# Moving one weight combination to another byte offset, and a smaller planner cost for a group of six products

## The chip, the cores and the metric

The kernel runs on one core of one Trainium2 chip, as one program. The metric is device time in microseconds (us) of one execution. Engines are named as in the profile: PE is TensorE's matmul, PEld its weight load, DVE is VectorE, ACT is ScalarE, POOL is GpSimd, SP is SyncE, which issues most DMAs.

## The reference

Retention attention, a one-expert-per-token feed-forward layer, and a dense feed-forward layer, in float32. The change is in the last, `_moe2_ref`, on 4608 tokens with a model width of 512 and 2048 hidden units:

```python
h = np.maximum(x @ w_in, 0.0)
return (h * h @ w_out).astype(np.float32)
```

## The kernel before

`phase0` does the attention, `phase12` the expert layer and, beside it, the preparation of the dense layer's weights (into `wc` in device memory); `phase3` does the dense layer.

**The dense layer.** Each 2x2 block product is done with seven products instead of eight (a Strassen-Winograd form), on seven combinations of the activations (`XT[0..6]`), of the first weights (`w`, `MW` says which) and of the second weights. Every operand is split into a high and a low part (`hilo`, `split`), and a product is taken as high x high, high x low, low x high. `six` issues such a group: two triples of matmuls, each with 128 rows, a 128x128 weight and 256 columns. Its three matmuls stand in lines 1210, 1211 and 1212: the first two use the same high weight, the third the low weight. The expert layer's counterpart is `three` (lines 839 to 841), with up to 512 columns and 256 in its last, narrowest tile.

**Order of the work.** `PASSES` cuts the 2048 hidden units into eight slices of 256, taken as three passes of 3, 2 and 3 slices. In each pass all nine tiles of 512 tokens are done (in alternating direction). For a tile and a slice q of the pass, `one` gives seven groups (x = 1, 2, 6, 5, 7, 4, 3 in that order for a slice; the slices overlap by the numbers in `AT1`), then come the squares on ACT and DVE and the splitting into `h`; `two` gives seven groups for each slice with `h` as the weight. That is 9 x (3 + 2 + 3) x 7 x 2 = 1008 groups, 6048 matmuls.

**The planner.** `Plan.add` records every operation with its engine, an assumed duration and the keys that it reads and writes; `Plan.emit` is a list scheduler. It puts a due time on each operation from the sum of the assumed PE durations, walks an assumed clock forward, and so fixes the order in which each engine's queue receives its work (and for the squares which of DVE and ACT does them). Nothing of the assumed times remains at run time: the engines run their queues in that order and wait on semaphores. The assumed duration of a group is `MMS`, 0.72 us; a DMA's is its size over 320 plus 2.0 us.

**Layout.** For the first weights one tile per slice and half (x = 0 high, x = 1 low) holds seven combinations of 256 columns (1024 bytes) in a row. The view starts 16 floats, 64 bytes, after the tile's start. The activations `XT`, which are the moving operand beside them, start at the tile's start. All these tiles start a whole number of 256 bytes apart. So within every 128 bytes the weights of `one` start 64 bytes off the moving operand. In `two` the weights are `h`, whose view starts 56 floats in so as to be 64 bytes off likewise, and the moving operand is the second weight at a tile's start. In the expert layer (`wx`, `wy` against `xh`, `hh`) weights and moving operand both start at byte 0 in this sense. Below, "byte 64" and "byte 0" name these two cases.

**Weights' transfers.** `wload2` loads the first pass's early slices at the end of `phase12`, `loadw` the rest. Each load of a first-weight tile is one DMA of 896 KB under one key, `("w", 0, q, x)`; a group of `one` waits for the keys of both halves.

Of the kernel before, what the change touches and what calls it, by code (L numbers as in the profile page):

```python
# [9 lines left out]
F32 = mybir.dt.float32  # L10
F32R = mybir.dt.float32r
# [14 lines left out]
P = 128  # L26
# [15 lines left out]
PASSES = ((0, 1, 2), (3, 4), (5, 6, 7))  # L42
# [50 lines left out]
def kernel(ctx, tc, qT, kT, kN, vN, modT, w_gate, mbias, w1, w2, w_in, w_out,  # L93
                              vdec_d, odec_d, mats_d, rows_d, out):
    nc = tc.nc
    pe, act, dve, pool, sp = nc.tensor, nc.scalar, nc.vector, nc.gpsimd, nc.sync
# [35 lines left out]
    wc = dram.tile([2, NFP, 2, P, 7 * 256], F32, name="wc")  # L132
# [933 lines left out]
    held = {}  # L1066

    def wload2(m, j, pool_, load=True):
        for x in range(2):
            if m:  # L1070
                held["w", m, j, x] = pool_.tile([P, 4, 2, 256], F32R, tag="w", name=f"w{m}{j}{x}")
                if load:
                    for a in range(2):
                        n = 4 - x
                        sp.dma_start(held["w", m, j, x][:, 0:n, a, :].bitcast(F32),
                                     wc[m, PASSES[0][j], a][:, x * 1024:x * 1024 + 256 * n]
                                     .rearrange("p (m c) -> p m c", c=256))
                continue
            wt = pool_.tile([P, 7 * 256 + 32], F32R, tag="w", name=f"w{m}{j}{x}")
            held["w", m, j, x] = wt[:, 16:16 + 7 * 256].rearrange("p (m c) -> p m c", m=7)  # L1080
            if load:
                sp.dma_start(held["w", m, j, x].bitcast(F32).rearrange("p m c -> p (m c)"), wc[m, PASSES[0][j], x])

    MX = {1: 0, 2: 1, 3: 2, 5: 3, 6: 4, 7: 5, 4: 6}
    MW = {1: 0, 4: 1, 2: 2, 5: 3, 6: 4, 7: 5, 3: 6}
# [71 lines left out]
    def phase3():  # L1157
        with ExitStack() as c2:
            ff = c2.enter_context(tc.tile_pool(name="ff", bufs=1))
            sb = lambda name, shape, dt=F32R: ff.tile(shape, dt, tag=name, name=name)  # L1160
            plan = Plan()
            for j in (1, 2):
                wload2(1, j, wp, False)
            WT = [[[held["w", m, j, x] for x in range(2)] for j in range(3)] for m in range(2)]
# [12 lines left out]
            PE_, ACT_, DVE_, POOL_, DMA_ = (Eng(n_, h_) for n_, h_ in  # L1177
                                            (("PE", pe), ("ACT", act), ("DVE", dve), ("POOL", pool), ("DMA", sp)))
# [5 lines left out]
            def copy(o, i, c, r, w, f=AF.Copy):  # L1184
                plan.add(a_(c), lambda e: e.activation(o, i, f), r, w)  # L1185

            def tt(o, a, b, op, c, r, w, engs=None):
                plan.add(engs or d_(c), lambda e: e.tensor_tensor(out=o, in0=a, in1=b, op=op), r, w)  # L1188

            def sq(z, c, k):  # L1190
                def go(e):
                    if e is act:
                        e.activation(z, z, AF.Relu)
                        e.activation(z, z, AF.Square)
                    else:
                        e.scalar_tensor_tensor(out=z, in0=z, scalar=0.0, in1=z, op0=ALU.max, op1=ALU.mult)  # L1196

                plan.add(d_(c) + [(ACT_, 2 * a_(c)[0][1])], go, k, k)

            def dma(o, i, kb, r, w, early=False):  # L1200
                plan.add(m_(kb), lambda e: (pool if early else e).dma_start(o, i), r, w, 2.0)
# [5 lines left out]
            def six(ps, pairs, first):  # L1207
                def go(e):
                    for n, ((lh, ll), (rh, rl)) in enumerate(pairs):
                        e.matmul(ps[n], lh, rh, start=first and n == 0, stop=False, skip_group_check=True)  # L1210
                        e.matmul(ps[n], lh, rl, start=False, stop=False, skip_group_check=True)  # L1211
                        e.matmul(ps[n], ll, rh, start=False, stop=True, skip_group_check=True)  # L1212
                return go

            MMS = [(PE_, 0.72)]

            def loadw(p, m, j0=0):
                for j, fp in list(enumerate(PASSES[p]))[j0:]:
                    for x in range(2):
                        if m:  # L1220
                            n = 4 - x
                            for a in range(2):
                                dma(WT[m][j][x][:, 0:n, a, :].bitcast(F32),
                                    wc[m, fp, a][:, x * 1024:x * 1024 + 256 * n].rearrange("p (m c) -> p m c", c=256),
                                    131 * n, [], [("w", m, j, x, a)])
                            continue
                        dma(WT[m][j][x].bitcast(F32).rearrange("p m c -> p (m c)"), wc[m, fp, x], 917,
                            [], [("w", m, j, x)])

            def xprep(n):  # L1230
                p, t = T3[n]
# [37 lines left out]
            def one(n, q, x):  # L1269
                p, t = T3[n]  # L1270
                if x == 1:
                    HS_[n, q] = cnt[0]
                    cnt[0] += 1
                u = HS_[n, q]
                X_, Y_, Z_ = (b_[:, 0:256] for b_ in (BX[u % 2], BY[u % 2], BZ))
                kx, ky, kz = ("X", u % 2), ("Y", u % 2), ("Z",)
                z, h = ZT[u % 3], HT[u % 3]
                kz_ = lambda *i: [("z", u % 3, j) for j in i]
                ps, kp = (X_, kx) if x in (1, 6, 7, 4) else ((Z_, kz) if x == 2 else (Y_, ky))
                w, m, mx = WT[0][q], MW[x], MX[x]  # L1280
                plan.add(MMS, six([ps, ps], [((w[0][:, m, P * k:P * k + P], w[1][:, m, P * k:P * k + P]),
                                              (XT[mx][:, 0, k, :], XT[mx][:, 1, k, :])) for k in range(2)],
                                  x in (1, 2, 5)),
                         [("w", 0, q, 0), ("w", 0, q, 1), ("x", mx, 0), ("x", mx, 1)], [kp])
                last = q == len(PASSES[p]) - 1
                if x == 1:
                    copy(z[:, 1, :], X_, 256, [kx], kz_(1))
                elif x == 2:
                    tt(z[:, 1, :], z[:, 1, :], Z_, ALU.add, 256, [kz] + kz_(1), kz_(1))
                    sq(z[:, 1, :], 256, kz_(1))  # L1290
                elif x == 6:
                    copy(z[:, 0, :], X_, 256, [kx], kz_(0))
                elif x == 7:
                    copy(z[:, 2, :], X_, 256, [kx], kz_(2))
                    tt(z[:, 2, :], z[:, 2, :], Y_, ALU.add, 256, [ky] + kz_(2), kz_(2))
                    sq(z[:, 2, :], 256, kz_(2))
                    if last:
                        hsplit(u, z, h, 0, 2, kz_)
                elif x == 4:
                    copy(z[:, 3, :], X_, 256, [kx], kz_(3), AF.Relu)  # L1300
                    copy(z[:, 3, :], z[:, 3, :], 256, kz_(3), kz_(3), AF.Square)
                    hsplit(u, z, h, 2 if last else 0, 3, kz_)
                elif x == 3:
                    tt(z[:, 0, :], z[:, 0, :], Y_, ALU.add, 256, [ky] + kz_(0), kz_(0))
                    sq(z[:, 0, :], 256, kz_(0))
                    tt(z[:, 4, :], z[:, 0, :], z[:, 2, :], ALU.add, 256, kz_(0, 2), kz_(4))
                    if last:
                        hsplit(u, z, h, 3, 4, kz_)
                    tt(z[:, 5, :], z[:, 4, :], z[:, 1, :], ALU.subtract, 256, kz_(4, 1), kz_(5))
                    hsplit(u, z, h, 4 if last else 3, 5, kz_)  # L1310
                    tt(z[:, 6, :], z[:, 1, :], z[:, 0, :], ALU.subtract, 256, kz_(1, 0), kz_(6))
                    tt(z[:, 7, :], z[:, 3, :], z[:, 5, :], ALU.subtract, 256, kz_(3, 5), kz_(7))
                    hsplit(u, z, h, 5, 7, kz_)

            def hsplit(u, z, h, a, b, kz_):
                rs = kz_(*range(a + 1, b + 1))
                ks = [[("h", u % 3, m, x) for m in range(a, b)] for x in range(2)]
                c = 256 * (b - a)
                plan.add(a_(c), lambda e: e.activation(h[:, 0, a:b], z[:, a + 1:b + 1], AF.Copy), rs, ks[0])  # L1319
                plan.add(d_(c), lambda e: e.tensor_tensor(out=h[:, 1, a:b], in0=z[:, a + 1:b + 1],  # L1320
                                                          in1=h[:, 0, a:b].bitcast(F32), op=ALU.subtract),
                         rs + ks[0], ks[1])
# [8 lines left out]
            def two(n, x):  # L1331
# [4 lines left out]
                for q in range(len(PASSES[p])):  # L1336
                    u = HS_[n, q]
                    h, m, w, mo = HT[u % 3], MH[x], WT[1][q], MO[x]
                    plan.add(MMS, six([ps[:, 0, :], ps[:, 1, :]],
                                      [((h[:, 0, m, P * b:P * b + P], h[:, 1, m, P * b:P * b + P]),  # L1340
# [108 lines left out]
```

## Time and profile before

| | |
|---|---|
| three runs | 1328.75, 1331.18, 1335.86 us (median 1331.18) |
| the profiled execution, its own time | 1336.03 us |
| its span, first to last instruction | 1334.2 us |
| mean granted TensorE clock | 0.995 |
| PE busy, PEld busy | 97%, 91% of the span |
| DVE, ACT, POOL busy | 77%, 47%, 9% |

The own time is the whole execution; the span is what the trace covers, 1.8 us less. Matmuls overlap each other in the pipeline, so a matmul's duration (280 ns) is longer than the distance from one start to the next, and a busy PE says nothing of its pace. The pace is read from starts.

### The profile page before, as it was taken

Reading aid. Unit: us, or ns where it says so; the run is one execution under the profiler, and the core shown is the slowest. Engines: PE = TensorE matmul, PEld = TensorE weight load, DVE = VectorE, ACT = ScalarE, POOL = GpSimd, SP = SyncE. Lnnn points to the kernel's source line nnn. Section 1 sums busy time; section 2 is a strip of 40 time slices with the busy share of each in tenths; the row PEclk is TensorE's granted clock in tenths of the full one; section 3 lists DMA queues with packets and bytes.
Section 4 is the critical chain, followed back from the end, with each engine's and each line's share of the span. In section 5 each row is a group of like instructions: output and inputs, shape, how many; then the busy total and the mean of one; then the engine's idle time right before and its main releaser. Section 6 shows DMA issues by size and latency. Waiting matters only on the chain.

```text
span 1334.2 us, 26978 instructions
## 1 busy us (share of the span) xinstructions
PE 1294.7 (97%) x10639; PEld 1209.6 (91%) x10639; DVE 1021.8 (77%) x2095; ACT 624.4 (47%) x1283; POOL 125.3 (9%) x170
## 2 busy tenths in 40 slices
PE   7999989999999999899999999999999999999997
PEld 6888877888888888899999999999999999999997
DVE  3877858878887887666888888858788777776765
ACT  2344444545445445455656566534334344443333
POOL 3222112101110110000000000000000011111121
PEclk9999999999999999899999999999999999999999
DMA  9998257787787877789555544778799766655551
GB/s 330 391 347 304 77 197 240 265 299 275 259 297 246 304 266 250 265 289 319 228 225 217 201 174 176 283 257 308 273 344 346 270 217 216 214 193 174 174 187 51
DMA packets 152499, 331.89 MB, mean 249 GB/s; under 512 B 15440, under 2 KB 67440, under 8 KB 152368
## 3 DMA queue, kind: packets, MB, share of 16 engines
q1 hardware_dynamic: 144752, 309.82, 65.5%
q0 software_dynamic: 5840, 19.14, 4.0%
q8 instruction: 85, 1.39, 0.4%
q10 hardware_dynamic: 1776, 1.17, 0.3%
q14 instruction: 46, 0.38, 0.1%
HBM read 222.33 MB, written 107.78 MB: 247 GB/s over the span
## 4 chain that ended last, share of the span: by engine, by line
PE 43%; DVE 10%; DMA 1%; issue 1%; POOL 0%; POOLq 0%; DVEq 0%
PE bank L1211 14%; PE bank L1210 14%; PE bank L1212 14%; DVE z L1188 4%; DVE h L1320 3%; DVE z L1196 1%; DVE x L1188 1%; DVE yr L1188 1%; DMA w<-wc 1%; DMA x<-xc 1%; PE bank L839 0%; PE bank L840 0%; PE bank L841 0%; POOL out L1327 0%; DVE oe L1188 0%
## 5 line engine op out<-in xcount | busy, mean ns | idle before, releaser
L1211 PE MATMUL bank<-x,w 128*128 128x256 f32 x1008 | 282.5, 280 | 4.2 <-DVE x L1188 4.2
L1210 PE MATMUL bank<-w,h 128*128 128x256 f32 x1008 | 282.1, 280 | 2.2 <-DVE oe L1188 1.6
L1210 PE MATMUL bank<-x,w 128*128 128x256 f32 x1008 | 281.9, 280 | 2.3 <-DMA x<-xc 2.3
L1212 PE MATMUL bank<-w,h 128*128 128x256 f32 x1008 | 282.1, 280 | 0.7 <-DVE h L1320 0.7
L1212 PE MATMUL bank<-x,w 128*128 128x256 f32 x1008 | 281.8, 280 | 0.9 <-DMA w<-wc 0.9
L1211 PE MATMUL bank<-w,h 128*128 128x256 f32 x1008 | 281.6, 279 | 0.0
L1185 ACT ACTIVATE z<-bank 128x256 f32<-128x256 f32 x288 | 108.6, 379 | 255.1 <-PE bank L1212 254.3
L1211 PEld LDWEIGHTS bank<-x,w 128*128 128x128 f32 x1008 | 189.3, 188 | 5.8 <-DVE x L1188 5.8
L1212 PEld LDWEIGHTS bank<-w,h 128*128 128x128 f32 x1008 | 191.9, 190 | 1.2 <-DVE h L1320 1.1
L1212 PEld LDWEIGHTS bank<-x,w 128*128 128x128 f32 x1008 | 191.9, 190 | 1.1 <-DMA w<-wc 1.1
L1210 PEld LDWEIGHTS bank<-w,h 128*128 128x128 f32 x1008 | 189.4, 188 | 2.9 <-DVE oe L1188 2.0
L1210 PEld LDWEIGHTS bank<-x,w 128*128 128x128 f32 x1008 | 189.4, 188 | 2.6 <-DMA x<-xc 2.5
L1319 ACT ACTIVATE h<-z 128x512 fp32r<-128x512 f32 (+2 forms) x270 | 158.2, 598 | 70.7 <-DVE z L1188 55.5
L1211 PEld LDWEIGHTS bank<-w,h 128*128 128x128 f32 x1008 | 189.3, 188 | 0.0
L1320 DVE TENSOR_TENSOR h<-z,h 128x512 fp32r<-128x512 f32 (+2 forms) x270 | 168.7, 647 | 7.5 <-ACT h L1319 7.5
L1188 DVE TENSOR_TENSOR z<-z,bank 128x256 f32<-128x256 f32 x216 | 89.1, 415 | 56.6 <-PE bank L1212 41.9
L839 PE MATMUL bank<-xh,wx 128*128 128x512 f32 (+3 forms) x320 | 119.5, 373 | 4.2 <-ACT xh L794 2.8
L839 PE MATMUL bank<-hh,wy 128*128 128x512 f32 (+3 forms) x320 | 122.7, 384 | 0.0
L840 PE MATMUL bank<-xl,wx 128*128 128x512 f32 (+3 forms) x320 | 119.3, 373 | 1.0 <-DVE xl L795 1.0
L840 PE MATMUL bank<-hl,wy 128*128 128x512 f32 (+3 forms) x320 | 119.9, 375 | 0.2 <-DVE hl L856 0.2
L841 PE MATMUL bank<-hh,wy 128*128 128x512 f32 (+3 forms) x320 | 119.7, 374 | 0.0
L841 PE MATMUL bank<-xh,wx 128*128 128x512 f32 (+3 forms) x320 | 119.2, 372 | 0.0
(185 smaller groups left out, 2127.0 us busy)
## 6 DMA issues: line engine op xcount, KB each, us to landing
x<-xc SPq DMA_DIRECT2D x112, 512.0 KB, 5.6
wr<-w SPq DMA_DIRECT2D x80, 512.0 KB, 4.4
xc<-x SPq DMA_DIRECT2D x63, 512.0 KB, 3.7
wc<-cwh SPq DMA_DIRECT2D x16, 896.0 KB, 5.8
wc<-cwl SPq DMA_DIRECT2D x16, 896.0 KB, 6.5
w<-wc SPq DMA_DIRECT2D x16, 896.0 KB, 7.8
pd<-oe SPq DMA_DIRECT2D x24, 512.0 KB, 3.9
xd<-xs SPq DMA_DIRECT2D x9, 1024.0 KB, 5.4
```

The source lines that it names most:

```text
L839: pe.matmul(ps, lh, rh, start=first, stop=False)
L840: pe.matmul(ps, lh, rl, start=False, stop=False)
L841: pe.matmul(ps, ll, rh, start=False, stop=last)
L1185: plan.add(a_(c), lambda e: e.activation(o, i, f), r, w)
L1188: plan.add(engs or d_(c), lambda e: e.tensor_tensor(out=o, in0=a, in1=b, op=op), r, w)
L1196: e.scalar_tensor_tensor(out=z, in0=z, scalar=0.0, in1=z, op0=ALU.max, op1=ALU.mult)
L1210: e.matmul(ps[n], lh, rh, start=first and n == 0, stop=False, skip_group_check=True)
L1211: e.matmul(ps[n], lh, rl, start=False, stop=False, skip_group_check=True)
L1212: e.matmul(ps[n], ll, rh, start=False, stop=True, skip_group_check=True)
L1319: plan.add(a_(c), lambda e: e.activation(h[:, 0, a:b], z[:, a + 1:b + 1], AF.Copy), rs, ks[0])
L1320: plan.add(d_(c), lambda e: e.tensor_tensor(out=h[:, 1, a:b], in0=z[:, a + 1:b + 1], in1=h[:, 0, a:b].bitcast(F32), op=ALU.subtract), rs + ...
```

## The change

In each pass's first weight tile (slice 0 of the pass) the seventh combination, which `one` uses for x = 3, is put 64 floats instead of 16 after where it would start, so it stands at byte 0 and the other six stay at byte 64. The tile is 32 floats longer. The load of such a tile becomes two DMAs, one of six combinations (768 KB) and one of the seventh (128 KB), each with its own key, and a group waits only for the part that it uses. Other slices keep one DMA. In the planner a group counts 0.685 us instead of 0.72.

```diff
-            wt = pool_.tile([P, 7 * 256 + 32], F32R, tag="w", name=f"w{m}{j}{x}")
-            held["w", m, j, x] = wt[:, 16:16 + 7 * 256].rearrange("p (m c) -> p m c", m=7)
+            held["w", m, j, x] = pool_.tile([P, 7 * 256 + 64], F32R, tag="w", name=f"w{m}{j}{x}")
             if load:
-                sp.dma_start(held["w", m, j, x].bitcast(F32).rearrange("p m c -> p (m c)"), wc[m, PASSES[0][j], x])
+                for a, b in spans(j):
+                    sp.dma_start(w0at(m, j, x, a, b).bitcast(F32), wc[m, PASSES[0][j], x][:, 256 * a:256 * b])
+
+    def spans(j):
+        return ((0, 7),) if j else ((0, 6), (6, 7))
+
+    def w0at(m, j, x, a, b):
+        o = 16 if j or a < 6 else 64
+        return held["w", m, j, x][:, o + 256 * a:o + 256 * b]
...
-            MMS = [(PE_, 0.72)]
+            MMS = [(PE_, 0.685)]
...
-                        dma(WT[m][j][x].bitcast(F32).rearrange("p m c -> p (m c)"), wc[m, fp, x], 917,
-                            [], [("w", m, j, x)])
+                        for a, b in spans(j):
+                            dma(w0at(m, j, x, a, b).bitcast(F32), wc[m, fp, x][:, 256 * a:256 * b], 131 * (b - a),
+                                [], [("w", m, j, x, a)])
...
-                w, m, mx = WT[0][q], MW[x], MX[x]
-                plan.add(MMS, six([ps, ps], [((w[0][:, m, P * k:P * k + P], w[1][:, m, P * k:P * k + P]),
+                m, mx = MW[x], MX[x]
+                w = [w0at(0, q, a, m, m + 1) for a in range(2)]
+                a = 6 if m == 6 and not q else 0
+                plan.add(MMS, six([ps, ps], [((w[0][:, P * k:P * k + P], w[1][:, P * k:P * k + P]),
                                               (XT[mx][:, 0, k, :], XT[mx][:, 1, k, :])) for k in range(2)],
                                   x in (1, 2, 5)),
-                         [("w", 0, q, 0), ("w", 0, q, 1), ("x", mx, 0), ("x", mx, 1)], [kp])
+                         [("w", 0, q, 0, a), ("w", 0, q, 1, a), ("x", mx, 0), ("x", mx, 1)], [kp])
```

## Rows read from the trace of the kernel before

**Rows 1.** The page's busy line: busy us, share of the span, instructions.
```profile
PE 1294.7 (97%) x10639; PEld 1209.6 (91%) x10639; DVE 1021.8 (77%) x2095; ACT 624.4 (47%) x1283; POOL 125.3 (9%) x170
```
**Rows 2.** Timeline of PE, end of the expert layer into the dense one: start, duration, instruction.
```profile
603.83 0.28 PE L839 MATMUL bank<-hh,wy 128*128 128x256 f32 x1
...
608.87 0.28 PE L839 MATMUL bank<-hh,wy 128*128 128x256 f32 x1
...
609.11 0.28 PE L841 MATMUL bank<-hh,wy 128*128 128x256 f32 x1
609.23 0.28 PE L1210 MATMUL bank<-x,w 128*128 128x256 f32 x1
...
609.58 0.28 PE L1210 MATMUL bank<-x,w 128*128 128x256 f32 x1
```
**Rows 3.** Timeline of PE in the second pass; 59 rows lie between.
```profile
1000.07 0.28 PE L1211 MATMUL bank<-x,w 128*128 128x256 f32 x1
...
1007.14 0.28 PE L1211 MATMUL bank<-w,h 128*128 128x256 f32 x1
```
**Rows 4.** Timeline of PE in the first pass; 59 rows lie between.
```profile
850.06 0.28 PE L1210 MATMUL bank<-w,h 128*128 128x256 f32 x1
...
856.86 0.28 PE L1210 MATMUL bank<-x,w 128*128 128x256 f32 x1
```
**Rows 5.** Stretches: busy us (count) of PE, PEld, DVE, ACT, POOL, then PEclk, DMA share, GB/s.
```profile
610.00:632.00 22.00, 22.00 (x189) 22.00 (x189) 17.06 (x40) 14.38 (x32) 0.10 (x1) 1.00 0.99 306
693.20:722.40 29.20, 28.86 (x254) 28.63 (x252) 25.72 (x56) 17.81 (x38) 0.00 (x0) 1.00 0.53 199
888.00:1027.00 139.00, 139.00 (x1181) 139.00 (x1182) 111.84 (x241) 56.11 (x124) 0.00 (x0) 1.00 0.86 310
1030.00:1044.00 14.00, 14.00 (x121) 14.00 (x121) 10.68 (x24) 4.73 (x10) 0.00 (x0) 1.00 0.75 260
1054.00:1317.00 263.00, 263.00 (x2235) 263.00 (x2235) 192.42 (x412) 116.12 (x270) 34.70 (x64) 1.00 0.54 191
```
**Rows 6.** Waits of PE from 609 us on: who, for whom, total us, times, longest.
```profile
PE bank L1211 <- DVE x L1188: 4.2, 8, 1.1
PE bank L1210 <- DMA x<-xc: 2.3, 1, 2.3
PE bank L1210 <- DVE oe L1188: 1.6, 2, 0.8
PE bank L1212 <- DMA w<-wc: 0.9, 1, 0.9
PE bank L1212 <- DVE h L1320: 0.7, 1, 0.7
PE bank L1210 <- ACT h L1319: 0.6, 1, 0.6
```
**Rows 7.** Timeline of PE around one of the eight waits for DVE x.
```profile
693.08 0.28 PE L1210 MATMUL bank<-x,w 128*128 128x256 f32 x1
...
693.69 0.38 PE L1211 MATMUL bank<-x,w 128*128 128x256 f32 x1 [0.34 <-DVE x L1188]
...
693.91 0.28 PE L1212 MATMUL bank<-x,w 128*128 128x256 f32 x1
```
**Rows 8.** Timeline of PE where the second pass begins.
```profile
885.26 0.28 PE L1212 MATMUL bank<-w,h 128*128 128x256 f32 x1
887.84 0.39 PE L1210 MATMUL bank<-x,w 128*128 128x256 f32 x1 [2.31 <-DMA x<-xc]
888.07 0.28 PE L1211 MATMUL bank<-x,w 128*128 128x256 f32 x1
```
**Rows 9.** Timeline of PE, first 256-column matmuls of the expert layer; eight rows lie between.
```profile
586.03 0.28 PE L839 MATMUL bank<-xh,wx 128*128 128x256 f32 x1
...
587.09 0.28 PE L839 MATMUL bank<-xh,wx 128*128 128x256 f32 x1
```
**Rows 10.** Issues of DMAs from 609 us on: engine, count, KB each, median us to landing.
```profile
x<-xc SPq DMA_DIRECT2D x112, 512.0 KB, 5.6
...
w<-wc SPq DMA_DIRECT2D x10, 896.0 KB, 7.7
```

## The prediction

> **What bounds the kernel now.** I read the page's busy line first, then the timeline of PE, the table of stretches, PE's waits and the DMA issues. The busy line shows PE at 97% of the span [rows 1]; the reader should not stop there, because the matmuls overlap and a busy PE can run at more than one pace. The pace is in the distance between starts. Three occur for the same matmul of 256 columns at the same granted clock of 1.00:
>
> - byte 0, in the expert layer's narrow tile: 42 matmuls from 603.83 to 608.87, 120.0 ns each [rows 2];
> - byte 64, "slow lock": 60 matmuls in 7.07 us, 117.8 ns each [rows 3];
> - byte 64, "fast lock": 60 matmuls in 6.80 us, 113.3 ns each [rows 4].
>
> A group of six therefore takes 0.720, 0.707 or 0.680 us. The old planner cost is the first, the new one lies between the other two. With PE busy without a break for 139 and 263 us in the second and third pass [rows 5], the pace of PE is what sets the end there. In the first pass there is one short wait per tile as well: eight waits for DVE's low parts of x, 4.2 us of idle time together [rows 6]. All of PE's waits in the dense layer add up to 10.3 us [rows 6].
>
> The pace does not wander: it stays for many tiles and changes only where PE's stream is interrupted. The dense layer begins without an interruption and is slow from its first groups [rows 2]; each of the eight waits for DVE x is followed by the fast lock (the tile behind one of them: 254 matmuls touch a stretch of 29.20 us that also holds 0.5 us of the wait, so 252 in 28.6 us, 113.5 ns [rows 5]); the 2.31 us wait at the start of the second pass [rows 8] is followed by the slow lock, which fills the three stretches from 888 us on (the first: 1181, less two that only overlap its edges, in 139 us, 117.9 ns [rows 5]).
>
> **The change, part by part.**
>
> *The byte-0 group itself.* Each of 27 tiles (three passes of nine) has one group x = 3 of the pass's first slice, 6 matmuls, 162 in all. At 120.0 instead of 113.3 ns they cost 162 x 6.7 = 1.1 us; against 117.8 ns, 0.4 us. I take 1.1.
>
> *What it does to the matmuls behind it.* This is the large term, and no row shows it directly. Slow-lock matmuls in the four long stretches are 189 + 1181 + 121 + 2235 = 3726, less the two or three per row that only overlap its edge, some 3716 [rows 5]. If all ran in the fast lock, this gives 3716 x 4.5 ns = 16.7 us (117.8 - 113.3). If instead all the others fell into the slow lock, 6048 - 3716 = 2332 x 4.5 = 10.5 us are lost. These are the two ends. Three things help to place the case. First, the slow lock of the second and third pass persists because nothing interrupts it; the change puts one irregularity in every tile. Second, the irregularities that the trace has in the first pass ended in the fast lock eight times of eight [rows 6], and a fast lock, once there, outlasts the tile. Third, against this: the one place where a byte-0 stream runs into a byte-64 stream without a wait ends in the slow lock at once (three matmuls from 609.23 to 609.58, 117 ns each [rows 2]). But that byte-0 stream had long been regular. A byte-0 stream that has just begun is not: the first nine starts there are 1.06 us, 117.8 ns each and not yet 120 [rows 9]. A group of six is shorter than that, so it leaves in another phase than the one at 609. I take the fast end, less 1.5 us for tiles that a wait puts into the slow lock up to their next byte-0 group (three such half tiles of about 110 matmuls at 4.5 ns each): 15.2 us gained.
>
> The Trainium skill speaks against all of this: "SBUF — State Buffer", section "Who interferes with whom", gives TensorE two independent read ports, one for the moving operand and one for weights, and says that PE never waits on anyone. By that the byte offset could neither cost nor give anything, and the sum would be the planner's term alone. The three paces above disagree with it, since 120.0 and 117.8 ns differ from 113.3 at the same clock and shape.
>
> *Two DMAs instead of one.* 896 KB take 7.7 us to land [rows 10]. Each pass has two more issues on SP, six in all. Early reuse helps a little: the six combinations come free when x = 4 of the last tile is done and not only after x = 3. The second pass's start waits 2.31 us, but for x, not for w [rows 8]; the third pass's start waits 0.9 us for w [rows 6]. So the gain is between 0 and 0.9 us. The loss is bounded by the same kind of wait, one more in each of two pass changes, 2 x 2.3 us. The extra issues are in front of the x loads on SP's queue, which take 5.6 us to land [rows 10]; what hides them is the second half of the tile. I take 0.
>
> *The planner's 0.685.* It changes no instruction of PE, only orders, and which of DVE and ACT does some squares. In the planner PE's 1008 groups shrink from 725.8 to 690.5 us; the actual pace in the fast lock is 1008 x 0.680 = 685.4 us. With 0.72 the planner thinks that DVE has more time than it has, which fits the wait for DVE x: PE would get there 0.11 us after 693.08 and starts at 693.69, and the restart costs one more slot (0.22 us to the next start [rows 7]), so each costs 0.61 + 0.22 - 2 x 0.113 = 0.60 us. With the nearer cost some of these may go. The gain is at most the 10.3 us of all waits plus 0.1 us of restart for each; the loss is bounded by one new wait of this kind in each of the 18 tiles that have none, 18 x 0.60 = 10.8 us. DVE has room on the whole: in a fast tile it is busy 25.7 of 29.2 us [rows 5]. In the second pass DMA runs at a share of 0.86 [rows 5], which becomes 0.86 x 117.8 / 113.3 = 0.89; that fits. I take 1 us of gain.
>
> *Sum*, against the profiled execution's own time of 1336.0: + 1.1 - 15.2 - 0 - 1.0 gives 1320.9 us. I predict 1320. The median of the three runs is 1331.2, 4.8 us under the profiled one; runs of one program can differ by which lock follows a wait, and an all-fast stream leaves nothing to differ, so 1320 stands for the median as well: 0.8% faster.
>
> **The rivals.**
>
> *A slow lock behind each byte-0 group.* For it: the entry at 609 us [rows 2]. Against it: the group is shorter than the settling [rows 9]. Then the fast tiles of the first pass are lost from x = 3 on, about three quarters of each: 0.75 x 10.5 = 7.9 us, plus 0.4 for the groups; the waits for DVE x may shrink by 1 us. 1336 + 7 = 1343 us. It decides if the first pass's matmuls stand at 117.8 ns after x = 3.
>
> *The group is only local.* The lock before it returns behind it, in either direction. Then the sum is 0.4 to 1.1 us for the groups and the planner's term: 1334 to 1338 us. For it: a lock outlasts much in this trace. This is also what the rule of the skill would give.
>
> *Fast, but paid back in waits.* PE saves 0.7 us in a tile of the second pass, and DVE or DMA turns it into a wait. For it: the wait in each tile of the first pass, where PE is fast [rows 7], and a DMA share of 0.89. If the 18 tiles of the other passes each wait 0.6 us as well, 10.8 us go back: 1331 us.
>
> **How the numbers follow.** About 0.5% (6.7 us) is what a measurement of this kernel can tell from no change, so faster is below 1324.5 and slower above 1337.8. Fast lock nearly everywhere: 0.57, its own range 1311 to 1328 from the planner's bounds on the good side and about half of the bad. Slow lock behind the groups: 0.20. Local only: 0.13. Paid back: 0.10. Of the first, 0.06 lie above 1324.5; of the second, 0.03 lie below 1337.8; of the third, 0.02 above. That gives faster 0.52, slower 0.17 + 0.02 + 0.03 for a bad order from the planner = 0.22, same 0.26. The range leaves out one in ten on each side: 1310 to 1343.
>
> **What would show each step.** PE's starts in the second and third pass: 113.3 ns apart if right, 117.8 if the lock stays. Weight loads and matmuls of lines 1210 to 1212 shorter on average than now. One group a tile near 120 ns. Stretches of 100 us there hold some 880 matmuls. PE's waits for DVE x fewer than eight. Wrong would be: any long stretch at 117.8 behind byte-0 groups (the lock's step failed), or new waits of PE in the second and third pass (the planner's or the DMA's).

## The result, and the profile after

| | before | changed |
|---|---|---|
| runs of the first comparison | 4, median 1330.39 us (1328.75 to 1335.86) | 4, median 1344.82 us (1341.00 to 1346.17) |
| profiled execution, own time | 1336.03 | 1346.17 |
| span | 1334.2 | 1344.4 |

The ratio is 1.0108, 95% interval 1.0072 to 1.0143: 1.1% slower. The forecast was 1320 (range 1310 to 1343), faster. The time lies near that of the first rival, 1343 us (a slow lock behind each byte-0 group), but in part by luck, as the account below shows.

The stretches of the changed kernel (columns as in [rows 5]) show it first. Line numbers have moved: 1217, 1218 and 1219 are the former 1210, 1211 and 1212.

```profile
860.00:890.00 30.00, 30.00 (x257) 30.00 (x256) 19.28 (x44) 14.72 (x31) 0.00 (x0) 1.00 0.65 228
920.00:1050.00 130.00, 130.00 (x1105) 130.00 (x1104) 105.97 (x226) 58.22 (x129) 0.00 (x0) 1.00 0.86 313
1080.00:1320.00 240.00, 240.00 (x2039) 240.00 (x2038) 180.22 (x390) 96.44 (x211) 35.78 (x64) 1.00 0.53 192
```

Less two that overlap the edges, 240 us hold 2037 matmuls: 117.8 ns each. The second and third pass are as slow as before, and now the end of the first pass is too (255 in 30 us, 117.6 ns), where the kernel before had 113.3 [rows 4].

The timeline of PE around the byte-0 group of one tile in the first pass shows how it comes about (start, duration, instruction):

```profile
675.64 0.28 PE L1217 MATMUL bank<-x,w 128*128 128x256 f32 x1
...
676.66 0.28 PE L1217 MATMUL bank<-x,w 128*128 128x256 f32 x1
...
677.38 0.28 PE L1217 MATMUL bank<-x,w 128*128 128x256 f32 x1
...
678.56 0.28 PE L1218 MATMUL bank<-x,w 128*128 128x256 f32 x1
```

Nine starts from 675.64 to 676.66: 1.02 us, 113.3 ns each, the fast lock. Six from 676.66 to 677.38, the byte-0 group and its hand-over: 717 ns in the trace's whole nanoseconds, 119.5 each. Ten from 677.38 to 678.56: 118 ns, the slow lock. There is no wait in it.

PE's waits from 608 us on (columns as in [rows 6]; the four largest) moved rather than went away:

```profile
PE bank L1219 <- DVE h L1330: 4.5, 8, 0.7
PE bank L1217 <- DVE oe L1195: 1.5, 2, 0.8
PE bank L1218 <- DMA w<-wc: 1.1, 1, 1.1
PE bank L1217 <- DMA w<-wc: 0.9, 1, 0.9
```

The eight waits for DVE's low part of x [rows 6] are gone; in their place are eight for DVE's low part of h, 4.5 us instead of 4.2. The second pass's start waits for w in two steps instead of for x [rows 8]. All of PE's waits together fell from 10.3 to 8.7 us, yet their price rose, as the next table shows: idle time alone does not hold the restarts, nor a lower clock behind a wait.

**Where the 10.1 us between the two profiled executions are.** I counted matmuls of the dense layer whose start follows the one before within 115.6 ns ("fast"), and summed all distances of 140 ns and more, less 116 ns for each ("gaps": waits with their restarts, and stretches at a lower clock).

| traced execution | own time | fast, of 6048 | gaps, us |
|---|---|---|---|
| before | 1336.0 | 2213 | 14.9 |
| changed | 1346.2 | 962 | 19.5 |

1251 fewer fast matmuls x 4.45 ns = 5.6 us, 4.6 us more in gaps: 10.2 us. In all, own time = 1331.0 - 0.00445 x fast + gaps. The 1331.0 is set so that this gives 1336.1 and 1346.2 for these two; it then holds within 0.4 us for eight of the other twelve traced executions below. The other four are 2.7, 2.1, -1.9 and 1.3 us off; three of them began the dense layer 2.4 and 2.1 us later and 1.9 us earlier than the two above (611.7, 611.4 and 607.1 us), the fourth holds 72 groups at another byte.

By pass, in the order of the matmuls (first, second, third):

| traced execution | fast | gaps, us |
|---|---|---|
| before | 2048, 132, 33 | 6.3, 6.5, 2.1 |
| changed | 662, 186, 114 | 10.7, 6.4, 2.4 |
| cost_alone (below) | 665, 72, 2187 | 10.9, 2.7, 3.0 |

Both losses lie in the first pass. The second and third pass of the traced kernel before were slow already, so that no byte-0 group could cost much there.

### The profile page after: what moved, and what is told of

Read it like the earlier page. It is cut to its first block, busy times and chain, and to the rows that moved or that the text cites. A ratio compares the mean times of both kernels' runs of the same rounds, so it can differ in the third digit from the quotient of the medians.

```text
span 1344.4 us, 26995 instructions
## 1 busy us (share of the span) xinstructions
PE 1305.9 (97%) x10639; PEld 1217.0 (91%) x10639; DVE 1027.9 (76%) x2107; ACT 622.5 (46%) x1259; POOL 126.5 (9%) x170
## 4 chain that ended last, share of the span: by engine, by line
PE 42%; DVE 10%; DMA 2%; issue 1%; POOL 0%; POOLq 0%; ACT 0%; SPq 0%
PE bank L1219 14%; PE bank L1217 14%; PE bank L1218 14%; DVE z L1195 4%; DVE h L1330 3%; DMA w<-wc 2%; DVE z L1203 2%; DVE yr L1195 1%; DVE x L1195 1%; DVE oe L1195 0%; POOL out L1337 0%; PE bank L839 0%; PE bank L841 0%; PE bank L840 0%; POOLq L1455 0%
## 5 line engine op out<-in xcount | busy, mean ns | idle before, releaser
L1195 DVE TENSOR_TENSOR oe<-oe,bank 128x512 f32<-128x512 f32 x97 | 66.7, 687 | 74.8 <-PE bank L1219 68.5
L839 PE MATMUL bank<-xh,wx 128*128 128x512 f32 (+3 forms) x320 | 119.5, 373 | 4.1 <-ACT xh L794 2.8
L841 PE MATMUL bank<-hh,wy 128*128 128x512 f32 (+3 forms) x320 | 119.5, 373 | 0.0
```

Source lines behind the costliest of these rows:

```text
L839: pe.matmul(ps, lh, rh, start=first, stop=False)
L841: pe.matmul(ps, ll, rh, start=False, stop=last)
```

## The experiments

Theory 1 after the result: the offset at which a group stands decides in which lock it hands the stream over, and byte 0 always hands over the slow one. The main rival: byte 0 is local, and the planner's new order moved the waits so that they leave the slow lock. The first two parts below ran on one chip, the third and the fourth on a chip each, all beside the kernel before, whose median there is given.

**1. The two parts alone.** `byte0_alone` is the changed kernel with this line as before:

```diff
-            MMS = [(PE_, 0.685)]
+            MMS = [(PE_, 0.72)]
```

> The byte-0 combination and its own DMA, with the planner's group at 0.72 us as before. Theory 1 (a byte-0 group always hands the stream over in the slow lock, 117.8 ns): all 27 byte-0 groups are followed by 117.8 ns; the first pass is fast only between a wait and the next byte-0 group; 1340 to 1346 us. Rival (the planner's new order moved the waits, and byte 0 is only local): the first pass stays in the fast lock as in the kernel before, some 2200 matmuls at 113.3 ns, 1329 to 1337 us.

`cost_alone` is the kernel before with this line as in the change:

```diff
-            MMS = [(PE_, 0.72)]
+            MMS = [(PE_, 0.685)]
```

> The planner's group at 0.685 us alone, the layout as before. Theory 1: a lock entered behind a wait lasts until the next wait, so the long stretches without waits in the second and third pass may stand in either lock; the first pass has its three waits a tile as in the changed kernel and is fast behind most of them to the next; over 1500 matmuls at 113.3 ns; 1325 to 1340 us. Rival: the order is what costs, so about the changed kernel's time, 1341 to 1346 us, with under 1100 matmuls at 113.3 ns.

The kernel before had a median of 1338.5 us here. byte0_alone: 1341.5 (1336.5 to 1343.3), ratio 1.0022 (1.0006 to 1.0037). All 27 byte-0 groups are followed by 117.8 ns, 10 of them entered from the fast lock. The traced execution has 1818 fast matmuls: eight waits for ACT's z, between a byte-0 group and the next one, gave back the fast lock in parts of the third pass, which theory 1 had not placed there. cost_alone: 1335.1 (1328.6 to 1344.7), ratio 0.9985 (0.9956 to 1.0013), not told from the kernel before. The traced one has 2924 fast matmuls: slow through the second pass, fast through the third, as the wait between them left it. Its first pass, expected fast behind most waits, is mostly slow without any byte-0 group: 161 matmuls in 19 us of a tile are 118.0 ns each, where the kernel before has 113.5 [rows 5].

```profile
667.00:686.00 19.00, 19.00 (x163) 19.00 (x163) 14.01 (x30) 9.24 (x20) 0.00 (x0) 1.00 0.69 248
```

Its runs spread over 16 us, those of byte0_alone over 7. So the rival that byte 0 is only local falls (byte0_alone, in the old order, has 400 fast matmuls in the first pass), but the rival's other half stands: the new order's waits leave the slow lock in the first pass too. In the traced pair either part, by these traces, would have lost the fast first pass by itself. Over its ten runs the planner's cost alone does not slow the kernel; the traced one won back in the third pass what it lost in the first.

**2. Other offsets.** byte0_alone with a place of its own for the seventh combination in each pass p; the offsets in floats 36, 40, 24 are bytes 16, 32, 96 within 128.

```diff
-    def w0at(m, j, x, a, b):
-        o = 16 if j or a < 6 else 64
+    def w0at(m, j, x, a, b, p=0):
+        o = 16 if j or a < 6 else (36, 40, 24)[p]
```

> As byte0_alone, but the seventh combination stands at byte 16 (of 128) in the first pass, byte 32 in the second, byte 96 in the third. Theory 1, in the form that the pace hangs on the distance of weights and moving operand within 128 bytes: the group's own pace differs by pass, and each offset hands over in a lock of its own, the same one in all nine tiles of its pass; if one of them hands over at 113.3 ns, that pass is fast as a whole and 6 to 11 us shorter than at 117.8. Rival (the rest of the stream goes on in the lock that it had): the locks before and behind the group are the same in each tile.

`offsets_b` has (28, 44, 20) there, bytes 112, 48, 80.

> As offsets_a with byte 112 in the first pass, byte 48 in the second, byte 80 in the third. The same theories: one lock for each offset behind the group (theory 1), or the lock that the stream had before it (rival).

One execution each: 1337.4 and 1337.3 us. What follows the nine groups of a pass, by the lock in which they were entered:

| byte | entered fast | entered slow |
|---|---|---|
| 16 | 6 of 6 left fast | 3 of 3 left fast |
| 32 | 9 of 9 left fast | none |
| 96 | 5 of 5 left fast | 0 of 4 |
| 112 | 8 of 8 left fast | 0 of 1 |
| 48 | 6 of 6 left fast | 1 of 3 |
| 80 | 2 of 2 left fast | 4 of 7 |

So theory 1 holds for byte 16 (always fast) as for byte 0 (always slow). Bytes 96 and 112 passed on the lock that they met, as the rival said, and 48 and 80 did both. "Each offset has a lock of its own" was too strong; 32 stayed open. The timeline of PE in offsets_a shows byte 16 turning a slow stream fast:

```profile
615.82 0.28 PE L1217 MATMUL bank<-x,w 128*128 128x256 f32 x1
...
616.17 0.28 PE L1217 MATMUL bank<-x,w 128*128 128x256 f32 x1
...
617.23 0.28 PE L1217 MATMUL bank<-x,w 128*128 128x256 f32 x1
...
617.57 0.28 PE L1217 MATMUL bank<-x,w 128*128 128x256 f32 x1
```

0.35 us for three before the group (which begins at 616.17), 0.34 for three from the fourth start behind it on. Neither kernel was fast in time: with 4684 fast matmuls offsets_a has 27.1 us of gaps. At a planner cost of 0.72 and with the split transfers, eight waits for ACT's z stand in the third pass (3.7 us here, 3.1 in byte0_alone).

**3. The same order at three offsets.** The decisive set: the changed kernel again, the changed kernel with the combination left at byte 64 (`o = 16`), and at byte 16 (`o = 16 if j or a < 6 else 36`). In these three every engine has the same instructions in the same order; only the address of 162 matmuls' weights (and where their DMAs land) differs. `byte16_cost072` has byte 16 and the old planner cost.

> The changed kernel itself once more, beside the kernels that it is compared with. Theory 1 (a byte-0 group always hands over in the slow lock): as measured, 1341 to 1346 us; the runs lie close together, since nearly all of the stream is slow in every run.

> The changed kernel with the seventh combination at its old byte 64: the same two DMAs, the same keys, the same planner cost and so the same order; only the byte offset of 162 matmuls' weights differs. Theory 1: 5 to 15 us faster than the changed kernel (1327 to 1338 us) and with a wider spread, because the long stretches take whichever lock the last wait left; at least 1500 matmuls at 113.3 ns in the profiled run. Rival (order and split loads cost, not the offset): within 3 us of the changed kernel.

> byte0_alone with the seventh combination at byte 16 instead of byte 0 in all three passes, planner cost 0.72. Theory 1: all 27 groups hand over at 113.3 ns, as the nine of the first pass in offsets_a did; over 4800 matmuls fast; a wait for ACT's z of some 0.7 us a tile stays in the third pass, as in offsets_a; 1325 to 1332 us. Rival (which lock follows is a matter of chance, byte 16 was lucky nine times): fast behind about half of the groups, 1333 to 1340 us.

> The changed kernel with byte 16 instead of byte 0, planner cost 0.685. Theory 1: all 27 groups hand over at 113.3 ns; the planner's cost is now near the real 0.680 us, so the second and third pass have no wait a tile; 1318 to 1328 us, over 15 us faster than the changed kernel. Rival for the planner's part (a cost near the real one moves waits but does not remove them): PE waits as much as at 0.72, within 3 us of byte16_cost072.

| kernel | median (range), us | ratio to before (1341.7) | fast | gaps, us |
|---|---|---|---|---|
| after_again, byte 0 | 1342.8 (1340.1 to 1344.5) | 1.0005 (0.9992 to 1.0019) | 1044 | 15.4 |
| split_cost_no_shift, byte 64 | 1337.1 (1331.7 to 1341.9) | 0.9972 (0.9949 to 0.9994) | 2558 | 16.5 |
| byte16_cost0685, byte 16 | 1331.3 (1329.8 to 1334.0) | 0.9924 (0.9904 to 0.9944) | 4565 | 20.0 |
| byte16_cost072, byte 16 | 1337.5 (1337.0 to 1338.7) | 0.9968 (0.9955 to 0.9980) | 4213 | 24.9 |

(Fast and gaps are of the one traced execution.) Byte 0 instead of byte 64 costs 5.7 us, with nothing else changed; byte 16 gives 5.8. All 27 byte-0 groups of after_again were left slow, all 54 of byte 16 fast (four of these, in byte16_cost072, only for the two last starts before a wait). split_cost_no_shift is as theory 1 expected, in time and in its wider spread. Its gain over byte 0 lies behind the first pass: 849 fast matmuls there against 766, and 1709 against 278 in the other two. The same 220 us stretch shows it, first after_again:

```profile
1080.00:1300.00 220.00, 220.00 (x1870) 220.00 (x1869) 164.27 (x357) 86.79 (x190) 31.30 (x56) 1.00 0.55 197
```

and byte16_cost0685:

```profile
1080.00:1300.00 220.00, 220.00 (x1908) 220.00 (x1908) 164.29 (x356) 86.92 (x193) 35.35 (x64) 1.00 0.53 190
```

The clock, DVE and DMA are alike, PE takes 38 more matmuls. The planner's cost matters once the stream is fast: 6.2 us between the last two rows of the table. In gaps it is an exchange: 13.2, 3.5 and 3.4 us in the three passes at 0.685, 6.8, 7.2 and 10.8 at 0.72. PE's waits of byte16_cost072,

```profile
PE bank L1217 <- ACT z L1192: 6.1, 8, 1.0
PE bank L1218 <- DVE x L1195: 4.4, 8, 1.2
```

are not in byte16_cost0685, which waits instead

```profile
PE bank L1219 <- DVE h L1330: 7.5, 11, 0.8
```

Both byte-16 kernels missed their expected 1325 to 1332 and 1318 to 1328 us: the hand-over was as expected, the gaps were larger, and waits behind a group still left 1267 matmuls of byte16_cost0685 slow.

**4. The kernel before, and better versions.** The median of the kernel before had been 1330, 1338 and 1342 us. `before_again` is that kernel with its trace; the others are byte16_cost0685 with another offset (`else 40`), another planner cost (0.70), and all slices' seventh combination at byte 16:

```diff
-        return ((0, 7),) if j else ((0, 6), (6, 7))
+        return ((0, 6), (6, 7))
...
-        o = 16 if j or a < 6 else 36
+        o = 16 if a < 6 else 36
...
-                a = 6 if m == 6 and not q else 0
+                a = 6 if m == 6 else 0
```

> The kernel before once more, with a trace of an execution beside the later kernels. Theory 1 (its time is set by which lock its waits happen to leave): an execution near 1340 us has some 1200 matmuls at 113.3 ns, one near 1330 us over 2500; 4.5 ns a matmul explain the difference, and the waits are the same. Rival (this chip is slower as a whole): the count is about 2200 as in the first trace and the waits or the expert layer are longer.

> The changed kernel with byte 32 instead of byte 0. In offsets_a byte 32 was only entered from the fast lock. Theory 1 (each offset hands over in its own lock): all 27 groups are followed by 113.3 ns whatever came before, and the time is that of byte16_cost0685, 1328 to 1335 us. Rival for byte 32 (it passes on the lock that it meets): groups entered at 117.8 ns are left at 117.8; 1333 to 1341 us.

> byte16_cost0685 with 0.70 in the planner. If the planner's gain comes from a cost that is near the real one, 0.70 lies between the two measured (PE's waits between 11 and 15 us, 1331 to 1337 us); if the order is a matter of luck, anything from 1325 to 1342 us.

> byte16_cost0685 with the seventh combination of every slice at byte 16, 72 groups instead of 27. Theory 1: a wait that leaves the slow lock is followed sooner by a group that hands over fast; of some 1270 slow matmuls half become fast (2.8 us), the 45 more groups cost 45 x 6 x 4.5 ns = 1.2 us: 1327 to 1333 us.

| kernel | median (range), us | ratio to before (1329.6) | fast | gaps, us |
|---|---|---|---|---|
| before_again | 1327.7 (1323.9 to 1338.8) | 1.0008 (0.9974 to 1.0043) | 4647 | 17.0 |
| byte32_cost0685 | 1328.4 (1326.7 to 1335.1) | 0.9992 (0.9962 to 1.0022) | 4601 | 18.4 |
| byte16_cost070 | 1324.9 (1323.4 to 1326.6) | 0.9960 (0.9930 to 0.9989) | 5190 | 16.4 |
| byte16_all_cost0685 | 1327.6 (1324.6 to 1331.2) | 0.9970 (0.9942 to 0.9999) | 5126 | 17.9 |

The program of the kernel before, traced twice, had 2213 fast matmuls once and 4647 the other time, with nearly the same waits (10.3 and 10.4 us): 2434 x 4.45 ns = 10.8 us less, 2.1 us more in gaps, and 8.4 us between the two executions. In the second trace the third pass was fast from its start, which the first trace had slow in [rows 5]:

```profile
1054.00:1300.00 246.00, 246.00 (x2172) 245.99 (x2171) 185.80 (x395) 109.24 (x259) 34.74 (x64) 1.00 0.58 206
```

2170 in 246 us, 113.4 ns each. So for these two executions theory 1 holds: the lock accounts for the difference, not a chip that is slower as a whole. Where the medians were 1338 and 1342 us the kernel before was not traced. Byte 32 left all 21 groups fast that it met fast, and 4 of 6 slow that it met slow: nearer to its rival, though not always, and not theory 1's lock of its own. Its time, 1328.4 us, lies in theory 1's range and shows nothing gained here. byte16_cost070 has the lowest median of all, below the expected 1331 to 1337 us although its waits (11.2 us) are as expected there, and at the edge of the 1325 to 1342 us of mere luck. It is faster than the kernel before by 0.4%, and its runs lie within 3.1 us where those of before_again lie within 15. It was run beside neither the changed kernel nor byte16_cost0685, whose ratio to the kernel before, on another chip, is lower (0.9924). So it is not shown that 0.70 does better than 0.685 or 0.72; in the traces it has more fast matmuls and fewer gaps than either. Whether more groups at byte 16 give more is likewise not shown: byte16_all_cost0685 ran on another chip than byte16_cost0685.

## Why the prediction was wrong, point by point

*What bounds the kernel* was right. PE's pace sets the end, there are three paces at one clock, and the price of a lock is 4.45 ns a matmul; the sum of that price and the gaps accounts for ten of fourteen traced times within 0.4 us, the other four as said above.

*The step that failed first* is the one in "What it does to the matmuls behind it": that a group of six is too short to settle, so that it leaves in another phase than the byte-0 stream at 609 us. The group does not need to settle. From its first start on, its matmuls are 119 to 120 ns apart (117 or 118 to the next group's first), entered from either lock, and all 81 byte-0 groups traced in three executions were left slow, 24 of them entered fast. The nine starts of [rows 9] were the wrong row: that stream came from matmuls of 384 columns, not from byte 64. The right row was shown and weighed down, the hand-over in [rows 2], which is the very same transition. An irregularity in general was taken for what a wait does; the eight of eight of [rows 6] spoke of waits alone, and even those are no rule: the kernel before goes through nearly the same waits with 2213 fast matmuls one time and 4647 another.

*The sign of the large term* was thus reversed. 15.2 us gained were forecast; in the profiled executions the lock cost 5.6 us, within the bound of 10.5. These 5.6 us cannot be put down to byte 0 alone: they lie in the first pass, and cost_alone lost as many fast matmuls there. What byte 0 does by itself is the 5.7 us between medians with the order held fixed. The first rival's 1343 us came near by luck: it had 8.3 us for the lock and the groups and 1 us less in waits, and the pair has 5.6 us and 4.6 us more in gaps.

*The byte-0 group itself*: 717 ns from its start to its successor's, against 0.720 forecast; right. Here and in the locks behind it the rule quoted from the Trainium skill ("SBUF — State Buffer", section "Who interferes with whom") does not describe what is measured: with the same order on all engines the offset alone moved the time by 11.5 us between byte 0 and byte 16.

*The planner's 0.685* was the second term that failed: 1 us of gain was taken, with bounds of 10.3 and 10.8 us. Alone it shows no gain that can be told (0.9985, 0.9956 to 1.0013). That the waits for DVE x would become fewer was right; that nothing would take their place was wrong: DVE's h took it, 4.5 us for 4.2, and with the restarts the first pass's gaps went from 6.3 to 10.7 us. The forecast looked for a loss in the second and third pass only. In a fast stream it is worth 6.2 us (byte16_cost072 to byte16_cost0685), which no step had.

*Two DMAs for one*: 0 was taken, with a bound of 4.6 us. The traced execution of the changed kernel waited for w at the second pass's start, 0.9 and 1.1 us, and lost more to the clock (below). after_again has no such wait, so this is no fixed cost of the change, and it was not tried by itself.

*The median*: the forecast set one execution's lock for the kernel's. The ratio 1.0108 is against runs of the kernel before that were mostly faster than its traced one; beside the set of its runs with a median of 1341.7 us the changed kernel is the same (1.0005). What the change did in both of its traces is to hold the stream slow (962 and 1044 fast matmuls); how much that costs hangs on the lock in which the kernel before happens to run.

*The chances*: 0.57 less 0.06 is 0.51, not 0.52; nothing else hangs on it.

## What to carry to other kernels

Where PE is the bound, read the distance between starts stretch by stretch, not its busy share, and look for two paces of one instruction at the same clock; then a kernel's runs can differ without a change in it, and one trace is not the kernel. A transition that a trace shows once, in the same order and without a wait, is better evidence for the same transition elsewhere than a rule made from other irregularities. When only one address is to be judged, keep the instruction order fixed: the planner's order alone moved these kernels by as much as the effect.

## What the runs showed of the hardware

The offset within 128 bytes between the weights and the moving operand changes not only the pace of the matmul (120.0 ns at 0; 113.3 or 117.8 at 64) but, at two of the offsets tried, sets the lock of the matmuls behind it: byte 0 left the slow lock 81 times of 81, byte 16 the fast one 90 times of 90 in the kernels with it in the first slice alone. What makes this so was not tried.

Two waits of PE close together were followed by a lower clock for some matmuls in the changed kernel. Timeline of PE, then stretches with the granted clock before the last two numbers:

```profile
896.88 0.28 PE L1219 MATMUL bank<-x,w 128*128 128x256 f32 x1
898.04 0.38 PE L1217 MATMUL bank<-w,h 128*128 128x256 f32 x1 [0.88 <-DMA w<-wc]
899.54 0.38 PE L1218 MATMUL bank<-w,h 128*128 128x256 f32 x1 [1.12 <-DMA w<-wc]
...
900.91 0.41 PE L1219 MATMUL bank<-w,h 128*128 128x256 f32 x1
901.13 0.41 PE L1217 MATMUL bank<-w,h 128*128 128x256 f32 x1
```

```profile
896.00:900.00 4.00, 2.00 (x15) 1.60 (x14) 1.83 (x5) 1.57 (x4) 0.00 (x0) 0.99 1.06 381
900.00:904.00 4.00, 4.00 (x24) 4.00 (x23) 3.27 (x8) 1.54 (x3) 0.00 (x0) 0.59 1.03 410
```

Behind waits of 0.88 and 1.12 us the granted clock falls to 0.59 of 2.4 GHz in the mean of 4 us, so most of that stretch ran at 1.2 GHz, and matmuls are 0.21 to 0.22 us apart instead of 0.113 or 0.118. In before_again one wait of 2.84 us was followed by the same (0.81 in 888 to 892 us, 0.77 in 892 to 896); behind the one of 2.31 us in the traced kernel before [rows 8] the clock stayed at 1.00 (888 to 892 us). This is the smaller part of the 4.6 us more in gaps: at the second pass's start they are 4.5 us instead of 2.8, and 4.4 us more lie in the first pass.
